# Which queue the last seven stores leave on, and in how many pieces

## The chip, the cores and the metric

The kernel runs on one core of one Trainium2 chip. Its time is the device time of one execution in microseconds (us), and the number that is compared is the median over several runs. The core has a matrix engine (TensorE, PE in the profile), a vector engine (VectorE, DVE), a scalar engine (ScalarE, ACT), GpSimd (POOL) and SyncE (SP). Stores to memory are DMAs. A DMA is issued by one of three engines, ACT, SP or POOL, on that engine's own queue, and its bytes are then moved by the core's 16 DMA engines.

## The reference

What is computed, for a batch of 8, with 8 heads, 1024 positions and head size 64:

```python
k_proj = np.einsum('ks,bhsd->bhkd', E, k)            # E, F: 64 x 1024
v_proj = np.einsum('ks,bhsd->bhkd', F, v)
attn   = softmax(scale * q @ k_proj^T)               # 1024 x 64 for each head
x      = (attn @ v_proj), heads side by side         # 8 x 1024 x 512
h  = np.maximum(x^T @ w_tok1, 0.0) @ w_tok2          # mixes the 1024 positions
u  = x + h^T
h2 = np.maximum(u @ w_ch1, 0.0) @ w_ch2              # 512 -> 1536 -> 512
out = u + h2                                         # 8 x 1024 x 512, float32
```

## The kernel before

All 8 batches run through one program. Each batch goes through attention, the token mix and the channel mix. The channel mix is cut into two blocks a batch, 16 in all; `up_set` makes the first product and the ReLU of a block and `down_block` (with `product` and `mm`, L1289) the second. Matrix products of 2 x 2 blocks are made with seven products in place of eight, so the sums of results in PSUM are put together by VectorE at the end.

One block of output is 128 partitions by 4 rows by 512 columns. The four rows of a partition are two pairs (`sh` 0 and 1), and the 512 columns are two halves (`dh` 0 and 1). A pair lies in one of three output tiles `o0`, `o1`, `o2`. The smallest unit that is stored is one row of a pair, one half: 128 partitions by 256 float32, 1 KB a partition, 128 KB.

The order of the instructions on every engine is written out by hand. Each operation is a job with a number, and the string `ORDER` names the jobs by two characters each in the order in which they are issued; each engine gets its own jobs in that order. Nothing is scheduled when the kernel is built, except that the framework gives each DMA on a hardware queue one of eight semaphores in turn (here called lanes 0 to 7), and that at the very end (L1560) SyncE waits for every lane, one after another in the order of the lanes, before the core's engines meet in a last barrier.

For all blocks but the last, a pair is stored whole, 512 KB, on POOL's queue. The last block (`last`, then `finish`) has an order of its own, because nothing comes behind it that could hide its stores. There VectorE adds the parts up in `add_u` (L1336) and `add_row` (L1381), and the stores leave in smaller units on the two hardware queues, those of SP and ACT (L1327 is the line of every store). In this text they are called:

- **S1**: pair 1, right half, both rows, 256 KB. On SP.
- **S2**, the big one of the change: pair 0, left half, both rows, 256 KB. Its last add is an `add_u` on 512 columns, VectorE's second one just before the last five `add_row`. On ACT.
- **S3** and **S4**: pair 1, left half, row 0 and row 1, 128 KB each. S3 on SP, S4 on ACT.
- **S5**: pair 0, right half, row 0, 128 KB. On SP.
- **S6a** and **S6b**: pair 0, right half, row 1, in two pieces of 128 columns, 64 KB each, because the last matrix product is cut in two so that its first half can be added while the second runs. S6a on ACT, S6b on SP.

In `ORDER` the jobs of S2, S6a and S6b stand at the very end (`YC`, `YP`, `YR`), so on ACT's queue S2 stands behind S4, although its add comes earlier, and S6a stands behind S2:

```python
store(0, (0,), queue=nc.scalar)                                                 # S2
store(1, (0,), t, queue=nc.scalar if t else nc.sync)                            # S3, S4
store(0, (1,), t, cut, queue=nc.scalar if (t, cut) == (1, 0) else nc.sync)      # S5, S6a, S6b
```

As built, the lanes are S1 2, S3 3, S5 4, S4 5, S2 6, S6b 7 and S6a 0.

Of the kernel before, what the change touches and what calls it, by code (L numbers as in the profile page):

```python
# [55 lines left out]
    "VqVcS-TwVmVtT0U0VuVoT1W1VhU1W2TaViVwVjVrVxU2W5VkWJW6VvWKTzVyT+WNT-V-W8W0VzU3WOW9W7VsU4WAV+WQTrWPTZWR"  # L56
    "WLWSW3WDU5W4X0TtWBWyWTTbWCXIWMWzWVW+WUTxWEX1TyWFU7U6U8WWX4W-U9UBWXWbUAWZX2XaX3UCX5WcXbUDXJX7WYXcWdWH"
    "X6XdWGXMX8WgXNX9WhXPXCXQXAXDXeWiWjXfWaXOXBXEXKXGWmXRXLWIWkXUWlWnXVXhWoWeXiXWXgWqXjWrXmWfXnXkXoXSWsXs"
    "XTWpWtXtXlXHUEXYWuXZXuXpWvXqXFX-XXX+WwXxWxXyXvY9XzXrY0XwY1Y4Y2Y3Y6Y5Y7YAYDY8YBYJYFYEYMYGYKYNYHYLYOYI"
    "YCYQYPYR"  # L60
)
SPOTS = (
    "3024101126436327273643040127120236363170420436171063240217145624732113405063774765765024721257605205"
# [124 lines left out]
def kernel(  # L188
# [13 lines left out]
    nc = tc.nc  # L202
    P = 128
# [45 lines left out]
    def bank(b):  # L249

        return banks[b.at] if b.span == 1 else psum[:, b.at : b.at + 2]
# [69 lines left out]
    def dve(cols, fn, ps=True, **kw):  # L321
        t = cols / 960 + 0.07 if ps else cols / 1920 + 0.07
        return pl.add("DVE", t, t + 0.09, fn, **kw)
# [18 lines left out]
    def sp(t, fn, **kw):  # L342
        return pl.add("DMA", t, t + 2.0, fn, **kw)
# [35 lines left out]
    for i in range(HWK):  # L379
        pl.add("SPQ", 1.6 + 1.1 * HWK, 1.6 + 1.1 * HWK, lambda: None, writes=[("kv32", i)], prio=-1001)  # L380
        if i:
            act(
                1024, lambda: nc.scalar.copy(out=v_sb[:, 0:2], in_=kv32[1]),
                reads=[("kv32", i)], writes=[("v", 0), ("v", 1)], prio=-100,
            )
        else:
            dve(
                1024, lambda: nc.vector.tensor_copy(out=k_sb[:, 0:2], in_=kv32[0]),
                reads=[("kv32", i)], writes=[("k", 0), ("k", 1)], prio=-100,
# [15 lines left out]
    for m in range(SETS):  # L405
        cs = slice(m * cw, (m + 1) * cw)
# [78 lines left out]
    for m in range(SETS):  # L485
        cs = slice(m * cw, (m + 1) * cw)
# [5 lines left out]
    for c in range(2):  # L492
        cs = slice(3 * c, 3 * c + 3)
# [760 lines left out]
    def down_block(j):  # L1254
# [26 lines left out]
        def o_key(sh, dh):  # L1281
            return ("o", os[sh], dh)
# [29 lines left out]
            return jobs  # L1312


        def store(sh, halves=(0, 1), t=None, part=None, queue=None):
            rows = slice(i * NJ + 2 * sh, i * NJ + 2 * sh + 2)
            rs = slice(0, 2)
            if t is not None:
                rows = slice(rows.start + t, rows.start + t + 1)
                rs = slice(t, t + 1)  # L1320
            cs = slice(halves[0] * DH, (halves[-1] + 1) * DH)
            if part is not None:
                cs = slice(cs.start + part * P, cs.start + (part + 1) * P)
            queue = queue or nc.gpsimd
            share = len(halves) / 2 / (1 if t is None else 2) / (1 if part is None else 2)
            sp(
                1.5 * share, lambda: queue.dma_start(out=out_v[b, :, rows, cs], in_=o_t[os[sh]][:, rs, cs]),  # L1327
                reads=[
                    o_key(sh, dh) + (() if t is None else (t,)) + (() if part is None else (part,)) for dh in halves
                ],  # L1330
                prio=None,
            ).early = True

        def add_u(dst, key, src, sh, dh):
# [22 lines left out]
        if last:  # L1357
            return finish(p6, product, add_u, store, bk, view, o_of, o_key)
# [7 lines left out]
        product(3, 5)  # L1366
        add_u(o_of(0, 1), o_key(0, 1), "y", 0, 1)
        store(0)
        product(4, 6)
        add_to(0)  # L1370
        store(1)

    def finish(p6, product, add_u, store, bk, view, o_of, o_key):
        dc = ub_t[0]

        def add_row(src, t, dst, key, part, part_key, cut=None):
            src += str(t + (cut or 0))
            cs = slice(0, DH) if cut is None else slice(cut * P, (cut + 1) * P)
            return dve(
                cs.stop - cs.start,  # L1380
                lambda: nc.vector.tensor_add(out=dst[:, t, cs], in0=bank(bk[src])[:, cs], in1=part[:, t, cs]),  # L1381
                reads=[part_key], writes=[key], uses=[bk[src]],
            )

        def follow(j, other):
            j.deps.add(other)

        pieces = ((0, None), (1, 0), (1, 1))
        p5 = product(5, 3)
        follow(p5[0], p6[1])  # L1390
        da, da_key = o_of(1, 1), o_key(1, 1)
        db, db_key = o_of(1, 0), o_key(1, 0)
        add_u(da, da_key, "y", 1, 1)
        da_w = [add_row("w", t, da, da_key, da, da_key, cut) for t, cut in pieces]
        follow(product(2, 4)[0], p5[2])
        for t in range(2):
            c22 = add_row("z", t, da, da_key, da, da_key)
        store(1, (1,), queue=nc.sync)
        follow(da_w[0], add_u(dc, ("ub", 0), "y", 0, 1))
        follow(add_u(db, db_key, "y", 1, 0), c22)  # L1400
        follow(add_u(o_of(0, 0), o_key(0, 0), "x", 0, 0), c22)
        store(0, (0,), queue=nc.scalar)
        p4 = product(4, 6)
        for t in range(2):
            add_row("z", t, o_of(1, 0), (*o_key(1, 0), t), db, db_key)
            store(1, (0,), t, queue=nc.scalar if t else nc.sync)
        p3 = product(3, 5)
        follow(p3[1], p4[1])
        for t, cut in pieces:
            add_row("w", t, o_of(0, 1), (*o_key(0, 1), t) + (() if cut is None else (cut,)), dc, ("ub", 0), cut)  # L1410
            store(0, (1,), t, cut, queue=nc.scalar if (t, cut) == (1, 0) else nc.sync)


    for hp in range(HP):
# [150 lines left out]
```

## Time and profile before

| | us |
|---|---|
| median of 3 runs | 417.33 (416.77 to 417.68) |
| the profiled execution, its own time | 417.44 |
| its span, first to last instruction | 415.7 |
| busy: PE / DVE / ACT / POOL | 406.6 / 355.8 / 221.7 / 66.7 |
| granted TensorE clock | 0.997 |

The span is the stretch that the profile covers; some 1.7 us of the execution lie outside it. Busy time is the time in which an engine computes; issuing a DMA does not count. Where the profile names an engine with a small q (SPq, ACTq), it shows the sequencer of that engine: its DMA issues and its waits. A DMA has three moments: its issue, the time in which its packets are moved, and its landing, when the last of the 16 DMA engines has raised its semaphore. DMA queue q1 is SP's, q10 is ACT's, and q8 and q14 bring in the engines' own instructions.

### The profile page before, as it was taken

To read this page: it belongs to the slowest core of one execution; us is meant where nothing else is said; L and a number is where in the kernel's file an instruction comes from. 1 tells how busy PE (TensorE), PEld (TensorE's weight loads), DVE (VectorE), ACT (ScalarE), POOL (GpSimd) and SP (SyncE) were. 2 spreads that over 40 slices of the span, in tenths; PEclk is the share of its full clock that TensorE was granted. 3 is DMA by queue.
4 is the path that set the end of the run, shared out by engine and by line. 5 is a ranking of instruction groups with operands and counts; after the bars stand their busy time and mean duration, and the time that the engine had idled before them with its cause. 6 is when DMAs were issued, how large, how long until landed. Compare 5 with 4: busy or idle time off the path is not lost.

```text
span 415.7 us, 9593 instructions
## 1 busy us (share of the span) xinstructions
PE 406.6 (98%) x3911; PEld 344.3 (83%) x3911; DVE 355.8 (86%) x773; ACT 221.7 (53%) x429; POOL 66.7 (16%) x105
## 2 busy tenths in 40 slices
PE   8899999999999999999999999999999999999994
PEld 4488888688888888888988899888888898998894
DVE  2389899779999998989889798989898899978775
ACT  1648883268636574474745555365552755344620
POOL 8553021023002300112000130014000001000010
PEclk9999999999999999999999999999999999999998
DMA  9999999896998797986947959783997212260124
GB/s 166 204 201 205 206 201 188 156 190 158 197 150 173 183 186 146 158 172 132 246 96 153 126 178 154 159 160 74 199 185 116 52 50 102 52 145 9 52 102 152
DMA packets 93899, 61.69 MB, mean 148 GB/s; under 512 B 59040, under 2 KB 89376, under 8 KB 93856
## 3 DMA queue, kind: packets, MB, share of 16 engines
q0 software_dynamic: 35088, 45.09, 54.9%
q1 hardware_dynamic: 58128, 15.27, 22.8%
q8 instruction: 30, 0.49, 0.5%
q10 hardware_dynamic: 640, 0.72, 0.5%
q14 instruction: 13, 0.11, 0.1%
HBM read 59.24 MB, written 16.78 MB: 183 GB/s over the span
## 4 chain that ended last, share of the span: by engine, by line
PE 90%; DMA 4%; DVE 2%; POOL 2%; issue 1%; ACT 0%; POOLq 0%; DVEq 0%; ACTq 0%
PE psum L1289 35%; PE psum L1180 34%; PE psum L875 4%; PE psum L991 4%; PE psum L672 3%; PE psum L521 3%; DMA k_sb<-in_k_dram 2%; PE psum L637 2%; DMA uT<-u 2%; PE psum L736 1%; PE psum L712 1%; PE psum L1060 1%; DVE u L1105 1%; POOL k_sb L358 1%; POOL v_sb L358 1%
## 5 line engine op out<-in xcount | busy, mean ns | idle before, releaser
L1289 PEld LDWEIGHTS <-G 128*128 128x128 bf16 x1356 | 130.0, 98 | 18.8 <-issue 3.9
L1289 PE MATMUL psum<-wc_sb,G 128*128 128x256 bf16 (+1 forms) x780 | 101.5, 271 | 0.0
L1180 PEld LDWEIGHTS <-wc_sb 128*128 128x128 bf16 x768 | 73.9, 98 | 10.7 <-issue 2.4
L1202 ACT ACTIVATE G<-psum 128x512 bf16<-128x512 f32 x96 | 56.2, 602 | 45.3 <-PE psum L1180 44.7
L1289 PE MATMUL psum<-wT,G 128*128 128x256 bf16 x576 | 75.6, 273 | 0.3 <-DVE o L1346 0.3
L1216 DVE TENSOR_TENSOR G<-G 128x512 bf16<-128x512 bf16 (+1 forms) x140 | 69.4, 515 | 0.8
L1180 PEld LDWEIGHTS <-wT 128*128 128x128 bf16 x576 | 55.3, 98 | 7.3 <-issue 0.6
L1180 PE MATMUL psum<-S,wc_sb 128*128 128x256 bf16 x384 | 56.2, 273 | 0.0
L1180 PE MATMUL psum<-S,wT 128*128 128x256 bf16 x384 | 56.0, 273 | 0.1
L1180 PE MATMUL psum<-uT,wc_sb 128*128 128x256 bf16 x384 | 55.5, 273 | 0.1
L1327 POOL DMA_DIRECT2D out_dram<-o x30 | 16.4, 546 | 213.6 <-DVE o L1336 173.4
L692 DVE TENSOR_TENSOR x_sb<-psum,rdn 128x256 bf16<-128x256 f32 (+1 forms) x88 | 46.7, 540 | 1.8
L1336 DVE TENSOR_TENSOR o<-psum,u 128x512 f32<-128x512 f32 x59 | 39.9, 681 | 3.7 <-PE psum L1289 3.3
L1208 ACT COPY ub<-psum 128x512 f32<-128x512 f32 x48 | 28.1, 588 | 23.5 <-PE psum L1180 18.5
L652 ACT ACTIVATE a<-psum 128x512 bf16<-128x512 f32 x64 | 34.9, 604 | 8.6 <-PE psum L637 7.9
L1161 DVE CUSTOM_DVE_ANT_0 G<-psum,ub 128x512 bf16<-128x512 f32 x48 | 32.7, 683 | 6.9 <-PE psum L1180 6.6
L1223 ACT COPY psum<-psum 128x512 f32<-128x512 f32 x48 | 27.6, 580 | 18.9 <-PE psum L1180 13.3
L1161 DVE CUSTOM_DVE_ANT_0 G<-psum,ua 128x512 bf16<-128x512 f32 x48 | 32.6, 684 | 5.3 <-PE psum L1180 4.4
L1208 ACT COPY ua<-psum 128x512 f32<-128x512 f32 x48 | 28.3, 589 | 14.0 <-PE psum L1180 13.6
L1180 PE MATMUL psum<-uT,wT 128*128 128x256 bf16 x192 | 28.7, 273 | 0.0
L358 POOL DMA_DIRECT2D v_sb<-in_v_dram x18 | 13.4, 745 | 76.2 <-PE psum L1180 25.9
L672 PE MATMUL psum<-vb,a 128*128 128x130 bf16 x256 | 25.6, 220 | 0.1
(102 smaller groups left out, 500.0 us busy)
## 6 DMA issues: line engine op xcount, KB each, us to landing
out_dram<-o POOLq DMA_DIRECT2D x30, 512.0 KB, 3.8
k_sb<-in_k_dram POOLq DMA_DIRECT2D x14, 512.0 KB, 10.9
v_sb<-in_v_dram POOLq DMA_DIRECT2D x14, 512.0 KB, 7.1
q_sb<-in_q_dram POOLq DMA_DIRECT2D x14, 512.0 KB, 8.9
wc_sb<-in_moe_w_ch_dram POOLq DMA_DIRECT2D x6, 256.0 KB, 11.5
wc_sb<-in_moe_w_ch_dram POOLq DMA_DIRECT2D x4, 384.0 KB, 13.6
k_sb<-in_k_dram POOLq DMA_DIRECT2D x4, 256.0 KB, 7.3
q_sb<-in_q_dram POOLq DMA_DIRECT2D x4, 256.0 KB, 7.5
```

The lines of the kernel that those rows point to most:

```text
L358: return lambda: nc.gpsimd.dma_start(out=dst, in_=src)
L652: lambda g=g, half=half, bk=bk: nc.scalar.activation(out=a_t[g][:, half], in_=bank(bk), func=ACT.Exp, scale=scale),
L672: nc.tensor.matmul(view()[:, k, c].rearrange("p i d -> p (i d)"), a_t[g][:, c, at : at + P], vb[:, g].rearrange("k i d -> k (i d)"), start ...
L692: lambda: nc.vector.tensor_tensor(out=x_sb[:, rows, g * P : (g + 1) * P].rearrange("p (n c) (i d) -> p n c i d", c=2, i=2), in0=view()[:, ...
L1161: nc.vector._custom_dve(TENSOR_ADD_SAT, out=out, in0=in0, in1=in1, s0=FMAX, s1=0.0)
L1180: nc.tensor.matmul(t[:, c, :], w1_of(n, dd, 2 * m + c), a_of(j, n, dd), start=(n in (1, 7) and c == 0 and dd == 0), stop=(c == 1 and dd == 1),
L1202: lambda: nc.scalar.activation(out=G[:, n, cs], in_=view(src), func=ACT.Relu),
L1208: 512, lambda: nc.scalar.copy(out=dst, in_=view("y")), writes=[(name, s % 2)],
L1216: 512 * len(both), lambda: f(out=G[:, n, c], in0=G[:, a, c], in1=G[:, b, c]), ps=False,
L1223: 512, lambda: nc.scalar.copy(out=view("y"), in_=view("x")), takes=[bk["y"]],
L1289: nc.tensor.matmul(to, G[:, G_OF[n], cc, t * P : (t + 1) * P], w2_of(n, cc)[:, cut], start=(n in opens and (t == 0 or alone) and cc == 0), ...
L1336: 512, lambda: nc.vector.tensor_add(out=dst, in0=view(src), in1=u_of(sh, dh)),
```

## The change

Three things, all in the last block. S2 goes from ACT's queue to SP's and its job moves ahead in `ORDER`, right behind S1, so that it leaves behind its own add. S3 goes from SP's queue to ACT's. S6a and S6b become one store, S6, of 128 KB on SP's queue, which waits for both adds. The adds and the matrix products stay as they are, in the same order.

```diff
-    "XTWpWtXtXlXHUEXYWuXZXuXpWvXqXFX-XXX+WwXxWxXyXvY9XzXrY0XwY1Y4Y2Y3Y6Y5Y7YAYDY8YBYJYFYEYMYGYKYNYHYLYOYI"
-    "YCYQYPYR"
+    "XTWpWtXtXlXHUEXYWuXZXuXpWvXqXFX-XXX+WwXxWxXyXvY9XzXrY0XwY1Y4Y2Y3Y6Y5Y7YAYDY8YBYCYJYFYEYMYGYKYNYHYLYO"
+    "YIYPYQ"
...
-        def store(sh, halves=(0, 1), t=None, part=None, queue=None):
+        def store(sh, halves=(0, 1), t=None, parts=(), queue=None):
...
-            if part is not None:
-                cs = slice(cs.start + part * P, cs.start + (part + 1) * P)
...
+            keys = [o_key(sh, dh) + (() if t is None else (t,)) for dh in halves]
...
+                reads=[k + (p,) for k in keys for p in parts] or keys, prio=None,
...
-        store(0, (0,), queue=nc.scalar)
+        store(0, (0,), queue=nc.sync)
...
-            store(1, (0,), t, queue=nc.scalar if t else nc.sync)
+            store(1, (0,), t, queue=nc.scalar)
...
-            store(0, (1,), t, cut, queue=nc.scalar if (t, cut) == (1, 0) else nc.sync)
+            if cut != 0:
+                store(0, (1,), t, () if cut is None else (0, 1), queue=nc.sync)
```

As built, SP then issues S1, S2, S5, S6 in this order and ACT issues S3, S4. The lanes are S1 2, S2 3, S3 4, S5 5, S4 6, S6 7.

More of the change, by code (lines that the diff above doesn't have):

```diff
@@ L1321, in store @@
             cs = slice(halves[0] * DH, (halves[-1] + 1) * DH)
-            if part is not None:
-                cs = slice(cs.start + part * P, cs.start + (part + 1) * P)
             queue = queue or nc.gpsimd
-            share = len(halves) / 2 / (1 if t is None else 2) / (1 if part is None else 2)
+            share = len(halves) / 2 / (1 if t is None else 2)
+            keys = [o_key(sh, dh) + (() if t is None else (t,)) for dh in halves]
             sp(
                 1.5 * share, lambda: queue.dma_start(out=out_v[b, :, rows, cs], in_=o_t[os[sh]][:, rs, cs]),
[L1328 to L1331, printed above, removed]
+                reads=[k + (p,) for k in keys for p in parts] or keys, prio=None,
             ).early = True
```

## The prediction

> **What bounds the kernel now.** I read the page first, then the chain of work that ended last in the final 21 us, then what SyncE waited for there. The page and the chain:
>
> ```profile
> span 415.7 us, 9593 instructions
> PE 406.6 (98%) x3911; PEld 344.3 (83%) x3911; DVE 355.8 (86%) x773; ACT 221.7 (53%) x429; POOL 66.7 (16%) x105
> ```
>
> ```profile
> 399.93 10.53 PE psum L1289 x108
> 410.46 0.02 issue
> 410.48 0.29 DVE o L1381
> ```
>
> TensorE is busy for 98% of the span, and the change touches none of its instructions. The chain ends with the last add at 410.48 + 0.29 = 410.77, yet the span goes on to 415.7: 4.9 us in which no engine computes. Only these, and the few us of adds before them, can be moved. What SyncE waits for in that time (columns: total, times, longest):
>
> ```profile
> SPq L1560 <- DMA out_dram<-o: 2.6, 1, 2.6
> ```
>
> So the tail is store issue, data, landing, and a closing sequence. The adds on VectorE and the issues of the seven stores, from the timeline (start, duration):
>
> ```profile
> 407.77 1.27 DVE L1336 TENSOR_TENSOR o<-psum,u 128x512 f32<-128x512 f32 x2
> 408.96 0.41 DVE L1381 TENSOR_TENSOR o<-psum,o 128x256 f32<-128x256 f32 x1
> 409.29 0.41 DVE L1381 TENSOR_TENSOR o<-psum,ub 128x256 f32<-128x256 f32 x1
> 409.81 0.42 DVE L1381 TENSOR_TENSOR o<-psum,o 128x256 f32<-128x256 f32 x1
> 410.15 0.62 DVE L1381 TENSOR_TENSOR o<-psum,ub 128x128 f32<-128x128 f32 x2
> ```
>
> ```profile
> 407.88 0.43 SPq L1327 DMA_DIRECT2D out_dram<-o  x1
> 409.40 0.34 SPq L1327 DMA_DIRECT2D out_dram<-o  x1
> 409.85 0.37 SPq L1327 DMA_DIRECT2D out_dram<-o  x1
> 410.27 0.35 ACTq L1327 DMA_DIRECT2D out_dram<-o  x1
> 410.66 0.46 ACTq L1327 DMA_DIRECT2D out_dram<-o  x1
> 410.80 0.33 SPq L1327 DMA_DIRECT2D out_dram<-o  x1
> 411.22 0.48 ACTq L1327 DMA_DIRECT2D out_dram<-o  x1
> ```
>
> In order these are S1, S3, S5, S4, S2, S6b, S6a. S2's add ends at 407.77 + 1.27 = 409.04, but S2 leaves at 410.66, behind S4. S6a's add ends near 410.43, but it leaves at 411.22, behind S2's issue. The DMA view of the last 21 us gives sizes and time from issue to landing:
>
> ```profile
> out_dram<-o SPq DMA_DIRECT2D x1, 256.0 KB, 2.4
> out_dram<-o SPq DMA_DIRECT2D x2, 128.0 KB, 1.8
> out_dram<-o ACTq DMA_DIRECT2D x1, 256.0 KB, 3.0
> out_dram<-o ACTq DMA_DIRECT2D x1, 128.0 KB, 1.8
> out_dram<-o SPq DMA_DIRECT2D x1, 64.0 KB, 2.3
> out_dram<-o ACTq DMA_DIRECT2D x1, 64.0 KB, 3.0
> ```
>
> S6a lands last, at 411.22 + 3.0 = 414.2; S2 lands at 413.7, S6b at 413.1. Next the table of stretches; its last two columns are the busy share of the DMA engines and GB/s:
>
> ```profile
> 409.00:409.50 0.50, 0.50 (x8) 0.44 (x5) 0.50 (x3) 0.00 (x0) 0.00 (x0) 1.00 1.03 344
> 408.80:409.70 0.90, 0.90 (x11) 0.81 (x10) 0.90 (x3) 0.00 (x0) 0.00 (x0) 1.00 0.87 291
> 409.70:410.20 0.50, 0.50 (x12) 0.50 (x11) 0.40 (x3) 0.00 (x0) 0.00 (x0) 1.00 0.00 0
> 410.20:413.10 2.90, 0.24 (x5) 0.07 (x2) 0.53 (x3) 0.00 (x0) 0.00 (x0) 1.00 0.86 273
> 413.10:413.40 0.30, 0.00 (x0) 0.00 (x0) 0.00 (x0) 0.00 (x0) 0.00 (x0) 0.65 0.00 0
> 413.40:413.70 0.30, 0.00 (x0) 0.00 (x0) 0.00 (x0) 0.00 (x0) 0.00 (x0) 0.50 0.05 14
> ```
>
> S1 alone runs the DMA engines full, at 344 GB/s. Then they stand idle for half a microsecond, and from 410.20 to 413.10 the other six stores, 768 KB, go at a mean of 273. After 0.3 us of nothing a last handful of packets follows. The DMA queues say what that is; the first row is of 412.8 to 412.9, the second of 413.4 to 413.7 (packets, MB, share of 16 engines):
>
> ```profile
> q14 instruction: 1, 0.01, 35.3%
> ```
>
> ```profile
> q10 hardware_dynamic: 9, 0.00, 4.7%
> ```
>
> One engine's instruction fetch took 0.353 x 0.1 us x 16 = 0.565 us on one DMA engine, and the nine packets of S6a on ACT's queue, shut out behind it, came from 413.4. The other 15 shares of S6a were through by 413.1. Last, SyncE's closing sequence in 414.0 to 414.75 (durations in ns, first and last start):
>
> ```profile
> L1560 SPq EVENT_SEMAPHORE x8: 28/28/28, 414.2 to 414.7; - x8
> L1560 SPq DRAIN x1: 13/13/13, 414.7 to 414.7; - x1
> ```
>
> The lanes are waited for one after another. The late store, S6a, sits on lane 0 as built, the first hardware lane in the list, so the remaining steps, some 0.06 us each, all come after its landing.
>
> **The change, part by part.** All times are of the profiled execution.
>
> *When the stores leave.* A store on an idle queue starts 0.03 us behind its add (add to 409.37 = 408.96 + 0.41, S3 at 409.40). So S2 leaves SP at 409.07 instead of 410.66, and its issue of 0.43 to 0.46 us ends by 409.53. S5's add ends at 409.70, so it leaves at 409.73; the wait that S2 adds on SP holds up nobody, since S5 is not ready. S3 leaves ACT at 409.40 as before: ACT has nothing else. S4 stays at 410.27. S6 needs both pieces' adds, until 410.77, and leaves at 410.80, where S6b left. ACT's last issue ends at 410.62 instead of 411.70, SP's at 411.13 as before.
>
> *When the data move.* From S1's issue to its first data went 0.92 us (407.88 to 408.80), from S3's 0.80 (409.40 to 410.20). I take 0.95 for S2 and 0.85 for the smaller ones: data are there for S2 from 410.02, S3 410.25, S5 410.6, S4 411.1, S6 411.65. At 344 GB/s 128 KB take 0.38 us and 256 KB 0.76. From 410.02 on the DMA engines then never run dry: S2, S3 and S5 last until 411.54, S4 until 411.92, S6 until 412.30. The whole 768 KB at 344 GB/s is 2.29 us, the same end. S1's 256 KB filled a stretch of 0.9 us, 0.14 more than its 0.76, so I add 0.2 and take 412.5. Bounds: 412.3 by the full rate, 412.9 by the mean rate of 273 (2.88 us from 410.02). Before, it was 413.1.
>
> *The merge alone.* Two pieces become one, on one queue. It removes one issue (0.48 us) from ACT, costs S6a's early departure, which it did not have (it left 0.42 us behind S6b), and halves the packets. I cost it at nothing beyond the sum above; if the half-size packets were the slow part, the end goes toward 412.3, which the bounds hold.
>
> *The fetch.* Its 0.565 us on one DMA engine stays somewhere. Which engine fetches the trace does not say; ACT's queue is the last to finish before it (411.70, fetch 1.1 to 1.2 later). If it is ACT's, it follows ACT's end, which comes 1.08 earlier, to about 411.8: still inside the stores. A DMA engine that is never dry ends late by whatever it was held, 0.5 us, so the last packets are through at 413.0. Bounds: nothing if the fetch falls outside the stores, 0.57 if wholly inside.
>
> *Landing.* S1's data were through by 409.70 and it landed at 410.3; S6a's last packets were in 413.4 to 413.7, landed 414.2. I take 0.6, so S6 lands at 413.6 instead of 414.2: a gain of 0.6, bounds 0.2 (end 412.9, fetch 0.5, landing 0.6 make 414.0) and 1.3 (412.3 and 0.6, no fetch).
>
> *The closing sequence.* As built the six stores take lanes 2 to 7 in the order of their jobs, so S6 sits on lane 7, the last in the list. By its landing the seven steps before it are done. That takes 7 x 0.06, about 0.45 us, from behind the last landing; bounds 0.4 and 0.5 by the row's rounding, and 0.2 if a store in the middle lands last.
>
> Sum: 0.6 + 0.45 = 1.05 us. The execution shown goes from 417.44 to 416.4; the median lies 0.11 below it, so I predict 416.3.
>
> **The rule against it.** The rows show S2 queued for 1.6 us behind other issues while the DMA engines were idle. The Trainium skill ("DMA: Bandwidth & Descriptors", Issuing engines are not separate DMA queues) says that DMAs from any engine run on the same 16 DMA engines and that several issuers save only the sequencer's time. By that rule the change of queue as such brings nothing and only the earlier departure counts; the trace agrees so far as both queues' packets shared the engines between 411.6 and 412.8:
>
> ```profile
> q10 hardware_dynamic: 323, 0.29, 73.1%
> q1 hardware_dynamic: 144, 0.07, 19.5%
> ```
>
> Its stricter reading is the second rival below.
>
> **The rivals.**
>
> *The fetch gets out of the way.* If it belongs to another engine than ACT and stays at 412.87, or falls behind the closing wait, it meets no packet: the data end at 412.5, S6 lands at 413.1. Gain 1.1 + 0.45 = 1.55: 415.8. For it: the fetch and S6a's tail touched by only 0.2 us. Against: ACT is the engine that stopped last. The Trainium skill ("Runtime: NRT & Kernel Launch", Instruction fetch mechanics) has each sequencer fetch the next page at block boundaries while it executes the current one; by that rule ACT's one instruction fewer can move the boundary past the barrier, and this rival holds. No row here tells which.
>
> *The stores were bound by their bytes.* If the 273 GB/s is what several stores together get, and not gaps from late issues, the data end at 412.9, with the fetch 413.4, landing 414.0: gain 0.2 + 0.45 = 0.65, and 0.4 if the list is not emptied either: 416.7 to 416.9. For it: two queues shared full engines for most of a microsecond. Against: 344 with S1 alone, the idle half microsecond, and six separate starts.
>
> *Slower: SP's queue takes its stores one at a time behind a 256 KB store.* Then S5 is issued only when S2 has landed, and S6 when S5 has. S2 needs 3.0 (its row beside other stores), to 412.07; S5 1.8, to 413.9; S6 1.8, to 415.7. That is 1.5 later than 414.2, less 0.45: plus 1.05, 418.4. It decides from the point where S6 leaves later than 410.80 + 1.05 = 411.85. Against it: S5 left at 409.85 while S3, on the same queue, landed only at 411.2; but no row shows a 256 KB store with another close behind it on SP.
>
> That the change doesn't do what it says is excluded by the built order of instructions, which has S1, S2, S5, S6 on SP and S3, S4 on ACT.
>
> **How the numbers follow.** A measurement of this kernel can tell about 0.2%, 0.83 us, from no change: faster means below 416.5, slower above 418.2. My forecast, 416.3, has 0.52, and its own range, 415.9 to 416.7, lies for a fifth above 416.5: 0.42 faster and 0.10 the same. The fetch out of the way has 0.25, all faster. Bound by bytes has 0.16, all the same. The slower rival has 0.07. Together 0.67 faster, 0.26 the same, 0.07 slower. The range goes from 415.5 (the second case less 0.3 for the run-to-run spread) to 417.0, and leaves out the slower rival and the edges of the others.
>
> **What would show it.** Right: S2 issued on SP near 409.07; the DMA engines full from 410.0 to 412.5 without a gap; S6 last to land, 413.1 to 413.7; one or two steps, not eight, between the last landing and SyncE's drain; the instruction packet on q14 near 411.8 to 412.4, with a few packets of S6 late behind it. Wrong: S5 or S6 issued later than 409.8 and 410.9; a mean rate again near 273 from the first data on; a last landing at or behind 414.0; TensorE's last product elsewhere than 410.46, since nothing ahead of the stores should change.

## The result and the profile after

The changed kernel takes 415.52 us (median of 6 runs, 414.88 to 415.86), the kernel before in the same series 417.35 (416.57 to 417.68). That is 1.83 us less; the ratio is 0.9958, interval 0.9945 to 0.9970. A second series gave 415.60 against 417.17, ratio 0.9961 (0.9946 to 0.9976). The change makes the kernel faster, by 1.6 to 1.8 us instead of the 1.05 that was forecast. The profiled execution took 415.69 us.

The page of the changed kernel and the end of its chain of work (start, length):

```profile
span 413.9 us, 9589 instructions
PE 406.4 (98%) x3909; PEld 344.4 (83%) x3911; DVE 355.9 (86%) x773; ACT 221.9 (54%) x429; POOL 66.8 (16%) x105
```

```profile
400.11 10.53 PE psum L1289 x108
410.63 0.02 issue
410.65 0.29 DVE o L1377
```

Nothing ahead of the stores has changed. The last add ends at 410.65 + 0.29 = 410.94, here 0.17 later than in the execution before. So I count from the end of the last add, and call what follows it the tail: 413.91 - 410.94 = 2.97 us, where it was 415.67 - 410.77 = 4.90. The tail is 1.93 shorter. What SyncE waits for in it (total, times, longest), against 2.6, 1, 2.6 before:

```profile
SPq L1557 <- DMA out_dram<-o: 0.6, 2, 0.3
```

The six issues from the timeline (start, duration); in order S1, S2, S3, S5, S4, S6:

```profile
408.05 0.42 SPq L1326 DMA_DIRECT2D out_dram<-o  x1
409.24 0.38 SPq L1326 DMA_DIRECT2D out_dram<-o  x1
409.58 0.35 ACTq L1326 DMA_DIRECT2D out_dram<-o  x1
409.90 0.34 SPq L1326 DMA_DIRECT2D out_dram<-o  x1
410.44 0.34 ACTq L1326 DMA_DIRECT2D out_dram<-o  x1
410.97 0.34 SPq L1326 DMA_DIRECT2D out_dram<-o  x1
```

```profile
out_dram<-o SPq DMA_DIRECT2D x2, 256.0 KB, 2.4
out_dram<-o ACTq DMA_DIRECT2D x2, 128.0 KB, 2.2
out_dram<-o SPq DMA_DIRECT2D x2, 128.0 KB, 2.2
```

S2 leaves at 409.24, 1.70 ahead of the last add's end; before it left at 410.66, only 0.11 ahead. The second fence has sizes and median time to landing: S2 lands at 409.24 + 2.4 = 411.6. S6, the last to leave, is the last to land, at 412.99, 2.05 behind the last add. Before, S6a landed 3.43 behind it. The table of stretches (last two columns: busy share of the DMA engines, GB/s):

```profile
409.90:410.10 0.20, 0.20 (x7) 0.20 (x5) 0.12 (x1) 0.00 (x0) 0.00 (x0) 1.00 0.00 0
410.10:412.50 2.40, 0.52 (x10) 0.34 (x7) 0.80 (x3) 0.00 (x0) 0.00 (x0) 1.00 1.01 330
412.50:412.70 0.20, 0.00 (x0) 0.00 (x0) 0.00 (x0) 0.00 (x0) 0.00 (x0) 1.00 0.05 10
```

The idle half microsecond between S1's data and the next has shrunk to 0.3 (409.88 to 410.18, around the first row), and the late handful of packets is gone: the five stores behind S1 run the engines full for 2.4 us at 330 GB/s (before 2.90 us at 273), and are through 1.64 behind the last add. The queues in 412.4 to 412.5 (packets, MB, share of 16 engines) show where the fetch went:

```profile
q1 hardware_dynamic: 28, 0.02, 56.6%
q14 instruction: 1, 0.01, 51.8%
```

It comes at 412.49, 1.54 behind the last add, where it shares its engine with the very last packets of S6. Last, the closing sequence in 412.9 to 413.12 (durations in ns, first and last start):

```profile
L1557 SPq EVENT_SEMAPHORE  x1: 28/28/28, 413.0 to 413.0; - x1
L1557 SPq DRAIN  x1: 13/13/13, 413.1 to 413.1; - x1
```

One step and the drain follow the landing, where eight steps followed it before. The tail by its parts (us from the last add's end):

| | before | after | difference |
|---|---|---|---|
| last landing | 3.43 | 2.05 | -1.38 |
| landing to SyncE's drain | 0.53 | 0.08 | -0.45 |
| drain to the end of the span | 0.94 | 0.84 | -0.10 |
| tail | 4.90 | 2.97 | -1.93 |

### The profile page after: what moved, and what is told of

Same layout as the page of the kernel before. It is cut to its first block, busy times and chain, and to the rows that moved or that the text cites. A ratio compares the mean times of both kernels' runs of the same rounds, so it can differ in the third digit from the quotient of the medians.

```text
span 413.9 us, 9589 instructions
## 1 busy us (share of the span) xinstructions
PE 406.4 (98%) x3909; PEld 344.4 (83%) x3911; DVE 355.9 (86%) x773; ACT 221.9 (54%) x429; POOL 66.8 (16%) x105
## 4 chain that ended last, share of the span: by engine, by line
PE 92%; DMA 4%; DVE 2%; POOL 1%; issue 1%; POOLq 0%; DVEq 0%
PE psum L1289 36%; PE psum L1180 35%; PE psum L991 5%; PE psum L875 4%; PE psum L672 3%; PE psum L521 3%; DMA q_sb<-in_q_dram 3%; PE psum L637 2%; DMA v_sb<-in_v_dram 1%; PE psum L712 1%; PE psum L1060 1%; PE psum L736 1%; DVE u L1105 1%; PE psum L1092 1%; PE psum L618 1%
```

## The experiments

Three series, each with the kernel before beside it (medians 417.55, 417.17 and 417.42). The theory: the gain is S2's early departure, then S6's place at the end of the list, and the fetch of one engine's instructions among the stores costs about half a microsecond. What was open is whose fetch it is, and which part of the change carries how much.

**The moves without the merge.** S2 and S3 as changed, S6a and S6b as before, with the `store` of the kernel before, which can cut a row in two.

```diff
-            if cut != 0:
-                store(0, (1,), t, () if cut is None else (0, 1), queue=nc.sync)
+            store(0, (1,), t, cut, queue=nc.scalar if (t, cut) == (1, 0) else nc.sync)
```

> The moves of the change without its merge: S2 early on SP, S3 on ACT, but S6a (ACT, behind S4) and S6b (SP) stay two stores of 64 KB. The last store, S6b, is on lane 0, the first hardware lane of the closing list. Theory (early departure, plus a closing list that empties only if the last lane lands last): the DMA engines run full from 410.1 to 412.6 as in the changed kernel and the last landing is near 413.0, but some 0.45 us of list steps come behind it again: 1.3 us faster than the kernel before, 0.4 to 0.5 slower than the changed kernel. Rival (the merge is what pays, since half-size pieces cost an issue and more packets): last landing at 413.5 or later, and at most 0.8 us faster than before.

Measured 415.98, 1.57 us under the kernel before, ratio 0.9962 (0.9948 to 0.9975). Its tail is 3.47; the last landing comes 2.10 behind the last add, and the list is walked in full behind it (closing sequence in 412.8 to 413.45):

```profile
L1560 SPq EVENT_SEMAPHORE  x8: 28/28/28, 412.9 to 413.3; - x8
```

So the moves bring the landing forward by all of the 1.38 but 0.05, and what the merge adds is the lane: by the tails, 3.47 - 2.97 = 0.50, of it some 0.45 in the list.

**The merge without the moves.**

```diff
-        store(0, (0,), queue=nc.sync)
+        store(0, (0,), queue=nc.scalar)      # YC again behind YI in ORDER
...
-            store(1, (0,), t, queue=nc.scalar)
+            store(1, (0,), t, queue=nc.scalar if t else nc.sync)
```

> The merge alone: S6 as one store of 128 KB on SP, lane 7, and the other stores as before (S2 on ACT behind S4 near 410.8, S3 on SP). Theory: S2's data still start only near 411.8, and with S6 beside them the engines are busy until 412.9, so the last landing is near 413.4; the last store is on lane 7 or 6, so the list is empty: 1.2 to 1.4 us faster than before, 0.4 slower than the changed kernel. Rival (S2's early departure carries the gain): no more than 0.6 us faster than before, with a last landing at 413.9 or later.

Measured 416.14, 1.41 under the kernel before, ratio 0.9964 (0.9949 to 0.9980). What SyncE waits for in the tail, and S2's row in 411 to 413.9:

```profile
SPq L1557 <- DMA out_dram<-o: 1.5, 1, 1.5
```

```profile
out_dram<-o ACTq DMA_DIRECT2D x1, 256.0 KB, 2.9
```

S2, still late on ACT, now lands last, 2.83 behind the last add, on the lane ahead of S6's; the tail is 3.82. The fetch comes at +2.21 and meets no packet. By the tails the moves gain 1.43 and the merge 1.08, in all 0.58 more than both together (1.93). A gain that either half brings and that can be had only once would explain it: the last packets no longer lie behind the fetch. Its size is measured below.

**S3 back on SP's queue**, the rest as changed.

```diff
-            store(1, (0,), t, queue=nc.scalar)
+            store(1, (0,), t, queue=nc.scalar if t else nc.sync)
```

> The changed kernel with S3 back on SP's queue, so that SP issues S1, S2, S3, S5, S6 and ACT only S4. Theory (the queue as such does not matter, only the time of departure): S3 leaves behind S2's issue, at 409.6 to 409.7, which is when its add is over anyway, S5 at 410.1; the DMA engines stay full because S2's data cover both, and the time is that of the changed kernel within 0.2 us. Rival (SP's queue is a bottleneck with four stores close together): S5 and S6 leave late and the time rises by 0.4 us or more.

Measured 415.67, ratio 0.9960 (0.9945 to 0.9975), against 0.9958 for the change: by the medians S3's queue is worth nothing that can be seen. This is the rule of the Trainium skill ("DMA: Bandwidth & Descriptors", Issuing engines are not separate DMA queues) that issuing from several engines saves only the sequencer's time, and so far the medians agree with it. In the profile S5, now behind S3's issue on the same sequencer, leaves 0.77 ahead of the last add instead of 1.04: a queue matters through what stands ahead of a store on it. The medians don't tell the whole, though: 5 of the 12 executions took 416.2 us or more, none of the 12 of the changed kernel as much as 416, and the profiled one is of the long ones (416.90). Its rows of 412.8 to 412.9 and of 413.3 to 413.8:

```profile
q14 instruction: 1, 0.01, 33.8%
```

```profile
q1 hardware_dynamic: 9, 0.01, 5.3%
```

The fetch comes 1.35 behind the last add, 0.19 earlier than in the changed kernel, and again shuts out a handful of packets; the last landing is at 2.74 and the tail 3.66, 0.69 longer than that of the changed kernel. So with one store more on SyncE the fetch falls among the last packets. Whether the long executions are all of this kind isn't shown, since one was profiled.

**S6 on lane 0, first try.** S1 is issued as two stores of a row each, which shifts the lanes by one.

```diff
-        store(1, (1,), queue=nc.sync)
+        store(1, (1,), queue=nc.sync, split=True)   # two dma_start, one for each row
```

> The changed kernel with S1 sent as two stores of 128 KB on SP in place of one of 256 KB, which moves every later store one lane on: S6, the last to land, is then on lane 0 and not on lane 7. S1's two issues are over before S2's add ends. Theory (the closing list): last landing at the same distance from the last add as in the changed kernel, about 2.05 us, and eight steps of 0.06 us behind it instead of one: 0.4 to 0.5 us slower than the changed kernel, 1.3 faster than before. Rival (the waits of lanes already raised cost nothing that counts, or the gain is all in the data): the same time as the changed kernel within 0.15 us.

Measured 416.58, 0.97 under the kernel before, ratio 0.9976 (0.9961 to 0.9990), where 1.3 was expected. The eight steps are there, but the added instructions also moved the fetch to 0.56 behind the last add, amid the stores, where it held an engine back (last landing 2.50). This run mixes two causes and settles neither. It suggests, though, that a store more on SyncE moves the fetch.

**Is it ACT's fetch?** In the kernel before, eight tiny copies on ACT, near 396 us, bring forward ACT's page boundary, the point among its instructions at which the next piece of them is fetched.

```diff
+        if j is act_jobs[-3]:
+            for _ in range(8):
+                nc.scalar.copy(out=pad, in_=zero32[:, :1])
...
```

> The kernel before with eight added copies of one column on ACT near 396, where ACT is idle. Nothing at the stores is changed; ACT only runs eight instructions further into its code by then. Theory (the late instruction fetch is ACT's, and in the kernel before it holds one DMA engine just when S6a's packets come): the packet on q14 moves ahead of the stores, to about 401 to 403; the last landing comes 2.95 us behind the last add instead of 3.43; 0.4 to 0.6 us faster than the kernel before. Rival (the fetch belongs to another engine, which reaches its last stretch of code at the end whatever ACT does): the packet stays near 2.1 us behind the last add, the time is that of the kernel before within 0.15 us.

Measured 417.22 against 417.17, ratio 1.0003 (0.9991 to 1.0014): nothing. Instruction packets in 400 to 404 and in 408 to 414.5:

```profile
q14 instruction: 1, 0.01, 0.6%
```

```profile
q14 instruction: 1, 0.01, 0.5%
```

ACT's fetch did move, to 401.26, but the packet among the last stores stayed, 2.08 behind the last add, and so did the late landing, at 3.39. My theory that it is ACT's fell.

**SyncE's fetch taken away.** In the kernel before, eight DMAs of 512 bytes inside the chip's memory, issued by SyncE near 375 us; eight leave every lane as it was.

```diff
+        if j is act_jobs[-8]:
+            for p in pads:                      # 8 of them
+                nc.sync.dma_start(out=p, in_=zero32[:, :1])
...
```

> The kernel before with eight added DMAs of 512 bytes, SBUF to SBUF, on SP near 390, where SP is idle; eight of them leave every store on its lane. Theory, after the runs so far (the fetch that held up S6a is SyncE's own, 1.1 to 1.4 us behind its 80th recorded instruction, which was the first of the closing waits): the packet on q14 moves ahead of the stores, the last landing comes at 2.95 us behind the last add instead of 3.43, and the kernel is 0.4 to 0.5 us faster than before. Rival (not SyncE's either, or the late packets have another cause): packet and time as before, within 0.15 us.

Measured 416.55 against 417.42, ratio 0.9982 (0.9972 to 0.9991). The queues in 377 to 379, and two stretches at the end:

```profile
q14 instruction: 1, 0.01, 1.2%
```

```profile
409.80:412.75 2.95, 0.29 (x6) 0.11 (x2) 0.57 (x3) 0.00 (x0) 0.00 (x0) 1.00 0.84 267
412.75:413.50 0.75, 0.00 (x0) 0.00 (x0) 0.00 (x0) 0.00 (x0) 0.00 (x0) 0.92 0.00 0
```

The fetch is at 377.66, no late packets are left, the last landing comes at 2.83 instead of 3.43, and the tail is 4.29, 0.61 shorter. So the fetch is SyncE's. And without it the stores of the kernel before still average 267 GB/s: that low rate was not due to the fetch, and it is gone (330) where S2 departs early.

**The same eight, and nine, in the changed kernel.** The ninth puts S6 on lane 0.

> The changed kernel with the same eight small DMAs on SP; all stores on their lanes. Theory: the fetch, 1.5 us behind the last add in the changed kernel, met the last packets of S6 on one engine only by a tenth of a microsecond, so that moving it away changes nothing: last landing at 2.0, the time of the changed kernel within 0.15 us. Rival (the fetch still cost something there): 0.2 us or more faster than the changed kernel.

> The same with nine small DMAs, which moves every store one lane on, so that S6 is on lane 0 and the fetch still out of the way. Theory (closing list): last landing at 2.0 us behind the last add as with eight, then eight steps of 0.06 us: 0.4 to 0.5 us slower than the kernel with eight. Rival (the list costs nothing; the loss with S1 in two stores was all the fetch): the same time within 0.15 us.

With eight 415.11, ratio 0.9946 (0.9935 to 0.9958); with nine 415.64, ratio 0.9963 (0.9951 to 0.9975). Closing sequence of the first in 413.1 to 413.4, of the second in 414.3 to 415.1 (its execution ran later ahead of the stores):

```profile
L1563 SPq EVENT_SEMAPHORE  x1: 28/28/28, 413.2 to 413.2; - x1
```

```profile
L1563 SPq EVENT_SEMAPHORE  x8: 28/28/28, 414.4 to 414.9; - x8
```

The last landing is at 2.03 and 2.04; the tails are 2.95 and 3.38. The lane alone is worth 0.44 in the profile and 0.53 in the medians. With these runs the tail comes apart, by one profiled execution each: from 4.90 to 4.29 the fetch (0.61), from 4.29 to 3.38 the departures and the merge (0.90), from 3.38 to 2.95 the list (0.44). In the medians of this series the steps are 0.87, 0.91 and 0.53.

**A fetch put back among the stores.** In the changed kernel, two of ACT's tiny copies bring ACT's own boundary into the tail.

> The changed kernel with two such copies on ACT near 396, which should bring ACT's fetch two instructions earlier in its code, from behind S4's issue to ahead of it. Theory: the packet on q14 comes 0.6 to 1.2 us behind the last add, in the middle of the stores, instead of 1.5, where they are all but through; one DMA engine ends 0.4 to 0.5 us late, the last landing is at 2.4 to 2.6 instead of 2.05, and the time is 0.3 to 0.5 us above the changed kernel's. Rival (not ACT's, or a held engine catches up): no change beyond 0.15 us.

Measured 416.05 against 415.60 for the changed kernel in the same series: 0.45 slower. The queues in 411 to 412.6:

```profile
q14 instruction: 2, 0.02, 5.6%
```

Two packets, ACT's at 1.18 and SyncE's at 1.53 behind the last add. The last landing is at 2.80, where 15 of the 16 engines had raised S6's semaphore by 2.07; the tail is 3.73, 0.76 longer. Since the changed kernel has SyncE's packet too, at the same place and at no cost, the added cost comes with ACT's: a fetch inside the stores does cost what the forecast had put it at, and by the profile somewhat more.

**S2 still earlier.** VectorE's add for S2 changes places with the one for the left half of pair 1.

```diff
-    ...Y7YAYDY8YBYCYJ...
+    ...Y7YBYDY8YCYAYJ...
```

> The changed kernel with S2's add and the add before it on VectorE (pair 1, left half) changed over, so that S2's add ends 0.6 us earlier; S3 needs both adds and leaves as before. S2 is then issued right behind S1's issue, at 1.7 + 0.6 = 2.3 us ahead of the last add in place of 1.7. Theory (from 410.1 on the changed kernel is bound by the bytes through the DMA engines): S1's and S2's data run without the gap of 0.25 us between them, the last data end 0.3 to 0.4 us earlier and so does the kernel: 0.3 to 0.4 us faster than the changed kernel. Rival (the end is set by S6 alone, its issue plus a fixed time to landing of 2.0 us, since S6 cannot leave earlier): the same time as the changed kernel within 0.1 us.

Measured 415.16, 0.44 under the changed kernel in its series; ratio to the kernel before 0.9953 (0.9938 to 0.9968). By its median it is faster than the changed kernel too, though the two intervals overlap. S2 leaves 2.21 ahead of the last add. SP's two stores of 128 KB (S5, S6), and the stretch from the end of the data on:

```profile
out_dram<-o SPq DMA_DIRECT2D x2, 128.0 KB, 1.9
```

```profile
411.98:412.50 0.52, 0.00 (x0) 0.00 (x0) 0.00 (x0) 0.00 (x0) 0.00 (x0) 1.00 0.06 16
```

The data end at 411.98, 1.45 behind the last add; what the row holds is the fetch alone, 8 KB at 412.23. S6 lands 1.86 behind the last add, the tail is 2.78: 0.19 gained in the profile, where 0.3 to 0.4 was expected. S6 took 1.83 from issue to landing, and stores of 128 KB took 1.8 in the kernel before too (S3, S5), so its own issue and travel are probably close to being the limit; no run tests that.

**The same with S6 in two pieces**, and seven of SyncE's tiny DMAs, which put S6b on lane 7.

> The two adds changed over on VectorE as in the run before, S2 on SP behind S1, S3, S4 and S6a on ACT, S5 and S6b on SP, S6 thus in two pieces of 64 KB again, and seven small DMAs on SP near 390, so that S6b is on lane 7 and the fetch of SP out of the way. Theory (the merge gave nothing by itself but the lane; a store of 64 KB on idle DMA engines lands sooner than one of 128 KB by 0.19 us, half of its 0.38 at 344 GB/s): last landing at 1.65 to 1.75 us behind the last add, 0.1 to 0.2 us faster than with the adds changed over alone, 2.0 to 2.2 faster than before. Rival (the merge as such pays): 0.1 us or more slower than with the adds changed over alone.

Measured 415.30, ratio 0.9948 (0.9936 to 0.9960), tail 2.86. The pieces on ACT and SP:

```profile
out_dram<-o ACTq DMA_DIRECT2D x1, 64.0 KB, 1.9
```

```profile
out_dram<-o SPq DMA_DIRECT2D x1, 64.0 KB, 1.7
```

S6a on ACT lands last, at 1.88, no earlier than the whole S6: it left only at 0.02, behind S4's issue, and took 1.86. S6b took 1.69, a little less than the whole S6 (1.83). So the landing of 1.65 to 1.75 that I expected missed. In the medians this kernel is 2.12 under the kernel before in its series, the one with the adds changed over 2.01: the intervals overlap, and a gain of the pieces isn't shown.

## Why the prediction was right, and by which steps

The direction and most of the mechanism were right, but the size only just: 415.52 lies 0.02 above the lower end of the range, 415.5, and outside the forecast's own 415.9 to 416.7. The range reached so far down only because of the rival in which the fetch gets out of the way. Of the signs, S2's departure, the full engines and the one step behind the last landing came. S6 landed earlier than the 413.1 to 413.7 that was given (412.99), the fetch came later than 411.8 to 412.4 (412.49), and no packets came late behind it. The landing came forward by 1.38 by the table, a little beyond the upper bound of 1.3.

*When the stores leave*: right. S2 left 1.70 ahead of the last add's end (409.07 against 410.77 was forecast, also 1.70); S5 and S6 left as soon as their adds were done.

*When the data move*: right. Without the fetch, data to the end at 1.73 behind the last add were forecast, 1.64 was measured; no gap from S2's first data on, 330 GB/s.

*The merge alone*: right at about nothing, 0.05 beside its lane.

*The fetch*: this step failed, and it is the mis-sized term. It had the fetch as ACT's, moved ahead into the stores, with 0.5 us of delay still paid. Copies on ACT did not touch it, DMAs on SyncE moved it away: it is SyncE's. The changed kernel's fetch comes at 1.54, when all but the last packets are through, and the last landing, 2.05, is as good as without it (2.03). So the 0.6 that the fetch cost before is gained, where the forecast still charged 0.5 for it. The size of a fetch among the stores was right (0.5 forecast; 0.61 and 0.45 to 0.76 measured), its owner and place were not. That the change escapes it is luck, not design: nothing in the change aims at SyncE's fetch, and with S3 back on SP it came 0.19 earlier and was met.

*Landing*: 0.6 us from the last data to the landing were forecast; it was 2.05 - 1.64 = 0.41. These 0.19, 0.09 from the data's end and the fetch's 0.5 are the 0.78 by which S6 landed sooner behind the last add than forecast: 2.05 instead of 2.83 (413.6 - 410.77).

*The closing sequence*: right, 0.45 forecast, 0.45 in the table and 0.44 with the lane alone changed.

*Not in the forecast*: 0.10 behind SyncE's drain. In the last barrier ACT's drain took longer before than after (first row before, second after):

```profile
L1560 ACTq DRAIN  x1: 126/126/126, 415.3 to 415.3; - x1
```

```profile
L1557 ACTq DRAIN  x1: 8/8/8, 413.4 to 413.4; - x1
```

ACT has one instruction fewer, so this may be ACT's own page boundary, and two runs bear it out. In the kernel before with the eight copies on ACT, which bring that boundary forward, the drain is short too (row below) and 0.84 follow SyncE's drain; with the eight DMAs on SyncE, which leave ACT as it was, it takes 127 ns and 0.94 follow.

```profile
L1566 ACTq DRAIN  x1: 8/8/8, 415.3 to 415.3; - x1
```

The sum: these 0.78 at the landing and 0.10 at the barrier on top of the forecast's 1.05 make the tail's 1.93.

The rivals. That the fetch gets out of the way (415.8) is what happened in the main: it is another engine's than ACT, though it did not stay at 412.87 but came at 412.49, just late enough. The Trainium skill's rule ("Runtime: NRT & Kernel Launch", Instruction fetch mechanics), that each sequencer fetches its next page at block boundaries, agrees with the tiny DMAs on SyncE moving the packet by 35 us; but its remark that the cost is mostly hidden does not hold for the kernel before, where it was 0.6 us. That the stores were bound by their bytes is refuted by 330 GB/s with stores on two queues. That SP's queue takes one store at a time is refuted by S5, which left at 409.90, 1.7 us before S2 landed.

What stays open: the tail of the changed kernel is the same with SyncE's fetch and without it (2.97 and 2.95), yet the kernel with the eight tiny DMAs is 2.31 under the kernel before, the changed kernel 1.57 and 1.83. These intervals overlap. In both profiled executions of the changed kernel, one in each of its series, the fetch comes at 1.53 to 1.54 and the tail is 2.97; whether other executions meet it isn't settled. The kernel with S3 back on SP shows how little room there is.

## What to carry to other kernels

At the end of a kernel, follow each of the last stores from its add to its issue: one that is ready but stands behind another's wait on the same sequencer can leave the DMA engines idle, and here that is what its queue cost, not the engine that issued it. Then ask where the last store to land stands in the closing list, and whether an instruction fetch lies among its packets; before putting a price on that fetch, find out by a few added instructions on each engine whose it is.

## What the runs showed of the hardware that was not expected

A single instruction fetch of SyncE, one packet on one of 16 DMA engines, made the whole kernel end 0.61 us later, since that engine's share of the last store waited behind it: by the 16 raises of its semaphore in the trace, 15 shares of S6a had landed by 2.95 behind the last add and the last came at 3.43, where without the fetch all 16 were in by 2.83. Where the fetch falls seems to go by the count of instructions on that sequencer: the two kernels with one store more on SyncE had it at 0.56 and 1.35 behind the last add, the changed kernel at 1.54, the kernel before at 2.10, and eight DMAs more brought it 35 us forward. This is inferred; the count was not varied one by one.
